# PSUM banks for the last four Q projection pieces of a fused linear-attention and gated-MLP block

## The chip, the cores and the metric

The kernel runs on one core of one Trainium2 chip. The metric is the device time of one execution in microseconds. A core has five instruction streams that run at the same time and meet through semaphores: PE (the matrix engine, with its weight loads listed apart as PEld), DVE (vector), ACT (scalar), POOL, and SP, which here only issues DMAs. Matmuls write into PSUM, which is used as eight banks of 128 partitions x 512 float32; DVE and ACT read the results out of it.

## The reference

`x` is 2048 tokens x 1024 features in bfloat16. The block is a linear attention with 32 heads followed by a gated MLP with 3584 hidden features, each behind a layer norm and each added to the residual:

```
phi(t) = where(t > 0, t + 1, exp(t)) + 1e-6
q, k, v = split(layernorm(x) @ wqkv)            # 32 heads of 32
num = phi(q) @ (phi(k)^T v)     per head
den = phi(q) . sum_s phi(k)     per head, + 1e-6
h   = x + (num / den) @ wo
n   = layernorm(h)
out = h + (relu(n @ W_gate) * (n @ W_up)) @ W_down
```

## The kernel before

**Order of the work.** The program is written as one list of operations per engine (`_Plan`). Every operation names the buffers that it reads and writes, and the planner derives the semaphore waits: a writer waits for all earlier readers and the writer of its buffer, a reader for its writer (lines 50 to 82). Each engine runs its list strictly in the order in which the code adds to it. A PSUM bank is one such buffer (`B_bank[0..7]`), so the first matmul into a bank waits for the engines that last read that bank. All matmuls are recorded at line 453 (`mm`).

**Banks.** `alloc_banks(pool)` (line 330) returns the bank of the given pool that was touched longest ago in program order; it looks at the order in which the program names the banks, not at when they come free. `GB0` is banks 0 to 3, `GB1` banks 4 to 7, `ALL` both.

**Stages.** Tokens are cut into 16 tiles of 128. First come the layer norms, the K projection (two column halves `h`), most of the Q projection, and the attention matrices, up to some 170 us. Tile t's Q piece of half h, `q_piece(t, h, pool)`, is eight matmuls of 128x512 into one bank (`q_mm`, line 629) and an evacuation `phi` in three steps: ACT takes the exponential out of the bank (line 513), DVE clamps it (line 515), and DVE reads the bank again and writes the larger of the two into `pq`, which lies in tile `R_Q` (line 518). The bank is free when the last of these has read it.

**Around the change.** Lines 1046 to 1052 run, in this order on PE: `a4` for token tiles 0 to 3 (two banks each, eight matmuls a bank; the attention output, evacuated by DVE at line 769 with the residual added, then the statistics of the second layer norm, the normalised tile `xn2` in `R_X` and its DMA transpose into `hnT`, line 778), the second half of Q piece (13, 1), and Q pieces (14, 0), (14, 1), (15, 0), (15, 1). Then the MLP begins with round r = 0 (line 1058). `g_unit(r, ft, pair)` (line 782) makes one block of 128 hidden features for 512 tokens: eight matmuls with gate weights into the first bank of its pair, eight with up weights into the second, ACT's relu out of the first (line 801), and DVE's product of both (line 803). The pairs alternate, `pair_of = [(0, 1), (2, 3)]`; the first unit takes banks 0 and 1. Its matmuls read `hnT` of all four tiles of the round, so they also wait for the four DMA transposes of `a4`, and for the first weight blocks. From there on 28 units, two output rounds `d_round` (line 812), and the same for r = 1 to 3 follow; `a4` of the tiles of the next round is put in among the units, on banks 4 to 7.

**Which banks the code gives before the change**, worked through `alloc_banks`: `a4` of tiles 0 to 3 take 5, 4, 3, 2, 0, 6, 7, 5; Q piece (13, 1) holds bank 1; pieces (14, 0), (14, 1), (15, 0), (15, 1) take 4, 3, 2, 0. The later `a4` calls of tiles 4 to 7 take 6, 7, 5, 4, 6, 7, 5, 4.

Of the kernel before, what the change touches and what calls it, by code (L numbers as in the profile page):

```python
# [132 lines left out]
def bass_sequential_preLN__linear_attn_block__glu_gated_reglu__prompt_kernel(  # L133
# [47 lines left out]
    with es:  # L181
# [447 lines left out]
        def q_mm(st, h, pool, b=None, dcs=range(NDC)):  # L629
            if b is None:  # L630
                (b,) = alloc_banks(pool)
            for dc in dcs:
                lhs, bl = (xcT[st][:, dc, :], B_xcT[st][dc // QC]) if st < NC else (xnT[:, st, dc, :], B_xnT[st][dc // HC])
                mm(bank(b), lhs, heads_ji(wq[:, dc, h * NW:(h + 1) * NW]), dc == 0, dc == NDC - 1,
                   [bl, B_wq[h][dc // QC]], B_bank[b], "q_%d_%d" % (st, h))
            return b

        def q_out(st, h, b):
            dst, wb, nm = pq[:, st, h * NW:(h + 1) * NW], [B_pq[st][h]], "q_%d_%d" % (st, h)
            if st < NC:  # L640
                phi_scaled(b, ln1_k[st], dst, wb, nm)
            else:
                phi(b, dst, wb, nm)

        def q_piece(st, h, pool):
            q_out(st, h, q_mm(st, h, pool))
# [218 lines left out]
        GB1 = [4, 5, 6, 7]  # L865
        ALL = GB0 + GB1
# [182 lines left out]
        touch_bank(q13b)  # L1049
        for st in (14, 15):  # L1050
            for h in range(NH):
                q_piece(st, h, ALL)


        BG = [4, 5, 6, 7]
# [78 lines left out]
```

## Time and profile before

| | |
|---|---|
| median of 3 runs | 819.53 us (819.50 to 820.45) |
| the profiled execution, its own time | 820.19 us |
| its span, first to last instruction | 818.4 us |
| granted PE clock | 1.00 |
| PE busy | 811.9 us, 99% of the span, 3960 matmuls |
| DVE busy | 330.5 us, 40% |
| ACT busy | 147.2 us, 18% |
| PE's share of the chain that ended last | 96% |
| DMA queue q1, share of 16 engines' span | 52.4% |

The span is one execution seen by the hardware profiler; what lies around it makes up the rest of that execution's own time. Busy time of PE counts each matmul from its start to its modelled end, and neighbours overlap, so it says that PE is hardly ever without work, not that it works at its peak. An engine's idle time matters only where it lies on the chain of waits that ends last.

### The profile page before, as it was taken

The page shows a single profiled execution, that of the slowest core. Times are in us where ns is not written, and L with a number is a line of the kernel's source. Part 1 is how long each engine was busy: PE and PEld are TensorE (multiplying, and loading weights), DVE is VectorE, ACT ScalarE, POOL GpSimd, SP SyncE. Part 2 cuts the span into 40 slices and gives each one's busy share as a digit, 9 for nine tenths or more (in the row PEclk, how much of TensorE's full clock was granted, in tenths as well). Part 3 has the DMA queues.
Part 4 walks back from the last instruction along what each step waited for, and adds up shares of the span by engine and source line. Part 5 has one row for each costly group of instructions (what it writes and reads, how often), then busy time and mean ns, then how long its engine had stood idle before and what let it go on. Part 6 is the DMA issues. An engine that isn't in the chain of part 4 may idle for free.

```text
span 818.4 us, 9813 instructions
## 1 busy us (share of the span) xinstructions
PE 811.9 (99%) x3960; PEld 369.7 (45%) x3960; DVE 330.5 (40%) x578; ACT 147.2 (18%) x241; POOL 25.5 (3%) x58
## 2 busy tenths in 40 slices
PE   9999999999999999999999999999999999999998
PEld 4444444444444444444444444444444444444444
DVE  7988566675546320155462110554521112211111
ACT  6554323242110110011101100111110001111000
POOL 1221000010000000000000000000000000000000
PEclk9999999999999999999999999999999999999999
DMA  8798000492666546547474655555665553543152
GB/s 238 162 226 211 13 0 1 89 321 55 188 171 168 142 150 197 175 110 229 115 181 142 214 167 171 134 163 141 154 200 166 177 173 107 181 128 103 52 178 79
DMA packets 155357, 122.28 MB, mean 149 GB/s; under 512 B 53936, under 2 KB 150192, under 8 KB 155312
## 3 DMA queue, kind: packets, MB, share of 16 engines
q1 hardware_dynamic: 155168, 121.62, 52.4%
q8 instruction: 31, 0.51, 0.3%
q14 instruction: 14, 0.11, 0.0%
q10 hardware_dynamic: 144, 0.03, 0.0%
HBM read 104.86 MB, written 4.19 MB: 133 GB/s over the span
## 4 chain that ended last, share of the span: by engine, by line
PE 96%; DVE 2%; issue 0%; ACT 0%; DMA 0%; POOL 0%; DVEq 0%; ACTq 0%; POOLq 0%
PE ps L453 96%; DVE st L477 1%; DVE R_Q L769 1%; DVE R_Q L518 0%; DMA R_X<-in_A_x_dram 0%; DVE E2t L515 0%; ACT Et L513 0%; PE ps L588 0%; ACT wo L464 0%; DVE mv L481 0%; DVE pks L837 0%; DVE E2t L566 0%; POOL rstd L490 0%; DVE R_Q L577 0%; DVE ve L487 0%
## 5 line engine op out<-in xcount | busy, mean ns | idle before, releaser
L453 PE MATMUL ps<-R_W,R_N 128*128 128x512 bf16 x1792 | 389.4, 379 | 1.8 <-DVE R_Q L518 1.8
L453 PEld LDWEIGHTS ps<-R_W,R_N 128*128 128x128 bf16 x1792 | 175.3, 98 | 213.5 <-DVE R_Q L518 2.3
L453 PE MATMUL ps<-R_K,R_V 128*128 128x512 bf16 (+1 forms) x924 | 194.1, 373 | 0.0
L803 DVE TENSOR_TENSOR R_V<-R_V,ps 128x512 bf16<-128x512 bf16 x112 | 77.0, 687 | 229.1 <-PE ps L453 229.1
L801 ACT ACTIVATE R_V<-ps 128x512 bf16<-128x512 f32 x112 | 66.9, 597 | 506.6 <-PE ps L453 506.6
L453 PEld LDWEIGHTS ps<-R_K,R_V 128*128 128x128 bf16 x924 | 89.3, 98 | 104.5
L837 DVE TENSOR_TENSOR pks<-ps,R_Q 128x512 bf16<-128x512 f32 (+2 forms) x33 | 20.2, 669 | 176.5 <-PE ps L453 176.5
L453 PE MATMUL ps<-R_K,R_N 128*128 128x512 bf16 x256 | 60.8, 379 | 0.0
L453 PE MATMUL ps<-wo,R_T 128*128 128x512 bf16 x256 | 57.4, 379 | 0.0
L453 PE MATMUL ps<-R_W,R_T 128*128 128x512 bf16 x240 | 56.5, 379 | 0.0
L453 PE MATMUL ps<-R_V,R_T 128*128 128x512 bf16 x224 | 51.0, 379 | 0.0
L513 ACT ACTIVATE Et<-ps 128x512 bf16<-128x512 f32 x58 | 33.9, 594 | 59.2 <-PE ps L453 40.7
L453 PEld LDWEIGHTS ps<-wo,R_T 128*128 128x128 bf16 x256 | 25.0, 98 | 30.2 <-ACT wo L464 0.2
L453 PEld LDWEIGHTS ps<-R_K,R_N 128*128 128x128 bf16 x256 | 24.8, 98 | 30.0 <-issue 0.5
L453 PEld LDWEIGHTS ps<-R_W,R_T 128*128 128x128 bf16 x240 | 23.5, 98 | 28.3
L490 POOL TENSOR_TENSOR rstd<-ve,neghalf 128x1 f32<-128x1 f32 x32 | 18.1, 565 | 562.4 <-DVE ve L487 556.1
L453 PEld LDWEIGHTS ps<-R_V,R_T 128*128 128x128 bf16 x224 | 21.7, 98 | 26.2 <-issue 0.2
L518 DVE SCALAR_TENSOR_TENSOR R_K<-ps,E2t 128x512 bf16<-128x512 f32 x30 | 20.8, 692 | 14.5 <-PE ps L453 13.8
L769 DVE TENSOR_TENSOR R_Q<-ps,x 128x512 bf16<-128x512 f32 x28 | 19.3, 690 | 16.0 <-PE ps L453 16.0
L515 DVE TENSOR_SCALAR E2t<-Et 128x512 bf16<-128x512 bf16 x58 | 16.9, 291 | 14.7 <-ACT Et L513 14.3
L477 DVE BATCH_NORM_STATS2 st<-R_Q 128x6 f32<-128x512 bf16 x32 | 22.2, 694 | 1.1
L622 DVE TENSOR_TENSOR pks<-pks,R_K 128x512 f32<-128x512 f32 x30 | 20.6, 687 | 0.5
(63 smaller groups left out, 233.5 us busy)
## 6 DMA issues: line engine op xcount, KB each, us to landing
R_N<-in_B_W_gate_dram SPq DMA_DIRECT2D x28, 1024.0 KB, 5.4
R_N<-in_B_W_up_dram SPq DMA_DIRECT2D x28, 1024.0 KB, 7.5
R_K<-in_B_W_down_dram SPq DMA_DIRECT2D x56, 512.0 KB, 3.8
R_X<-in_A_x_dram SPq DMA_DIRECT2D x16, 256.0 KB, 3.0
out_dram<-pks SPq DMA_DIRECT2D x31, 128.0 KB, 3.8
x<-in_A_x_dram SPq DMA_DIRECT2D x14, 256.0 KB, 2.8
R_V<-in_A_wqkv_dram SPq DMA_DIRECT2D x8, 256.0 KB, 6.0
R_V<-in_A_wqkv_dram SPq DMA_DIRECT2D x2, 1024.0 KB, 5.9
```

The costliest lines, as they stand in the source:

```text
L453: lambda e: e.matmul(out_ap, lhsT, rhs, start=start, stop=stop, skip_group_check=skip),
L477: PL.add("dve", lambda e: e.bn_stats(out=st6[:, k, c * 6:(c + 1) * 6], in_=src[:, c * BCH:(c + 1) * BCH]), reads=[chunk_bufs[c]], writes=[ ...
L490: PL.add("pool", lambda e: e.tensor_tensor(out=rstd[:, k, :], in0=ve[:, k, :], in1=neghalf[:], op=ALU.pow), reads=[B_ve[k], B_neghalf], wr ...
L513: PL.add("act", lambda e: e.activation(out=Et[:, k, :], in_=src, func=ACTF.Exp), reads=[B_bank[b]], writes=[B_E[k]], name=name + "_exp")
L515: PL.add("dve", lambda e: e.tensor_scalar(out=E2t[:, k, :], in0=Et[:, k, :], scalar1=1.0, scalar2=1e-6, op0=ALU.min, op1=ALU.add), reads=[ ...
L518: PL.add("dve", lambda e: e.scalar_tensor_tensor(out=dst_ap, in0=src, scalar=C1, in1=E2t[:, k, :], op0=ALU.add, op1=ALU.max), reads=[B_ban ...
L622: PL.add("dve", lambda e: e.tensor_tensor(out=pks[:, c], in0=pks[:, c], in1=pk[:, st, :], op=ALU.add), reads=[B_pk[st], B_pks[h]], writes= ...
L769: PL.add("dve", lambda e, b=b, n=n: e.tensor_tensor(out=hsb[:, hs, j, n * NW:(n + 1) * NW], in0=bank(b), in1=x2t[:, n * NW:(n + 1) * NW], ...
L801: PL.add("act", lambda e: e.activation(out=rg[:, k, :], in_=bank(ga, SBW), func=ACTF.Relu), reads=[B_bank[ga]], writes=[B_rg[k]], name="rg ...
L803: PL.add("dve", lambda e: e.tensor_tensor(out=hhT[:, ft, :], in0=rg[:, k, :], in1=bank(gb, SBW), op=ALU.mult), reads=[B_rg[k], B_bank[gb]] ...
L837: PL.add("dve", lambda e: e.tensor_tensor(out=outst[:, k, c0:c1], in0=bank(b, c1 - c0), in1=hsb[:, hs, j, dh * NW + c0:dh * NW + c1], op=A ...
```

## The change

The pool of the last four Q pieces becomes banks 4 to 7 in place of all eight:

```diff
@@ -1049,7 +1049,7 @@
         touch_bank(q13b)
         for st in (14, 15):
             for h in range(NH):
-                q_piece(st, h, ALL)
+                q_piece(st, h, GB1)
```

By `alloc_banks` the pieces (14, 0), (14, 1), (15, 0), (15, 1) now take banks 4, 6, 7, 5 in place of 4, 3, 2, 0, and the `a4` calls of tiles 4 to 7 inside round 0 take 4, 6, 7, 5, 4, 6, 7, 5 in place of 6, 7, 5, 4, 6, 7, 5, 4. No later allocation differs. No instruction is added or removed on any engine, and none changes its place in its engine's order; only bank addresses and semaphore waits differ. On PE two waits move: the first matmul of unit 0 of round 0 keeps its waits for the four transposes and the gate weights, but has none left for ACT and DVE; the first matmul of the same unit's up half, which waited for its weights alone, now waits for ACT and DVE too.

## The prediction

> **What bounds the kernel now.** I read the page's first two parts, then the chain of waits, then PE's waits over time, then the timeline around the one place that these name. The page first:
>
> ```profile
> span 818.4 us, 9813 instructions
> ...
> PE 811.9 (99%) x3960; PEld 369.7 (45%) x3960; DVE 330.5 (40%) x578; ACT 147.2 (18%) x241; POOL 25.5 (3%) x58
> ...
> PE 96%; DVE 2%; issue 0%; ACT 0%; DMA 0%; POOL 0%; DVEq 0%; ACTq 0%; POOLq 0%
> ```
>
> PE is the bound: 96% of the chain that ended last is matmuls. A change of bank can only shorten the run where PE stands still, so the question is where that is. The list of who waited for whom, on PE from 100 us to the end, has one entry:
>
> ```profile
> PE ps L453 <- DVE R_Q L518: 1.8, 1, 1.8
> ```
>
> One stop, 1.8 us, for DVE's last step of `phi`. The chain in order of time puts it:
>
> ```profile
> 190.78 0.31 DVE E2t L515
> 191.11 0.70 DVE R_Q L518
> 191.88 0.60 ACT Et L513
> 192.50 0.30 DVE E2t L515
> 192.83 0.70 DVE R_Q L518
> 193.58 621.41 PE ps L453 x2900
> 815.07 0.44 DVE pks L837
> ```
>
> Up to 193.58 the chain runs through the evacuation of the last Q pieces; from there 621.41 us of matmuls follow without a break, then the last store. So whatever brings the matmul at 193.58 forward brings the end forward by as much. The timeline of PE and its neighbours there:
>
> ```profile
> 187.29 1.23 SPq L778 DMA_TRANSPOSE R_W<-R_X  x1
> ...
> 191.88 0.60 ACT L513 ACTIVATE Et<-ps 128x512 bf16<-128x512 f32 x1 [1.13 <-DVE R_Q L518]
> 192.50 0.29 DVE L515 TENSOR_SCALAR E2t<-Et 128x512 bf16<-128x512 bf16 x1 [0.70 <-ACT Et L513]
> 192.83 0.69 DVE L518 SCALAR_TENSOR_TENSOR R_Q<-ps,E2t 128x512 bf16<-128x512 f32 x1
> 193.58 2.49 PEld L453 LDWEIGHTS ps<-R_W,R_N 128*128 128x128 bf16 x13 [2.28 <-DVE R_Q L518]
> 193.58 2.76 PE L453 MATMUL ps<-R_W,R_N 128*128 128x512 bf16 x12 [1.79 <-DVE R_Q L518]
> ```
>
> The matmul at 193.58 (`R_W` is `hnT`, `R_N` the weight ring) is unit 0 of round 0. It wants bank 0, which piece (15, 1) has just filled; PE must wait for that piece's exponential (191.88 to 192.48), clamp and last read (to 193.52).
>
> **What the change removes.** Piece (15, 1) goes to bank 5, so bank 0's last reader is `a4` of tile 2, first half, the fifth of the eight adds at line 769; in the DVE timeline it starts at 179.52 and takes 0.69 us, over by 180.21. Bank 1, for the up half, is read last by `phi` of piece (13, 1), the first of the five after the norm: 187.50 plus 0.69 is 188.19. Both are done before PE wants them, and the wait of 1.79 us has no bank left to stand on. The exponential, clamp and read still take place, beside the first matmuls of unit 0.
>
> What PE gets is more than the 1.79 us, since that counts from the modelled end of the last Q matmul, and neighbours normally overlap. Pitch: the timeline merges the first 100 matmuls of the MLP to 21.76 us; less one matmul's 0.379, over 99 intervals, 0.216 us. The last Q matmul ends at 193.58 - 1.79 = 191.79 and began at 191.41. With nothing to wait for the next begins at 191.41 + 0.216 = 191.63. Gain: 193.58 - 191.63 = 1.95 us.
>
> **What stands behind the wait.** Unit 0 also reads `hnT` of four tiles and the first weights. The latest transpose is issued at 187.29 (above); the DMA view of 187 to 188.5 us has its landing:
>
> ```profile
> R_W<-R_X SPq DMA_TRANSPOSE x1, 3.6
> ```
>
> 187.29 + 3.6 is 190.9. PE's weight loads run one matmul ahead of their matmuls, so the wait is met at about 191.63 - 0.22 = 191.41: 0.5 us to spare. The same view of the three transposes before gives 4.8 for the first and 3.0 for the third. I take 3.6, the row of this very transfer; bounds are 3.0 (nothing changes) and 4.8, landing at 192.1, which costs 0.7 us. The gate and up weights were issued between 160.18 and 167.4, and the longest median landing of such a block around there is 10.1 us; they are in.
>
> **What it adds.** Four pieces in banks 4, 6, 7, 5 must find these free. Their last readers are the adds of `a4`, tiles 0 (second half), 2 (second half), 3 and 3, which by the DVE timeline end at 175.1, 181.5, 183.4 and 184.8. The pieces start, eight pitches (1.73 us) apart and ending with the one whose last matmul began at 191.41, at 184.72, 186.45, 188.17 and 189.90. Spare: 9.6, 4.9, 4.8 and 5.1 us; cost nothing. If that cover were gone, each late us would stop PE for one.
>
> Next in line: ACT's relu of unit 0 becomes ready 1.95 earlier than 195.57, at 193.62, when the last exponential is over (192.48). DVE's product, at 197.41 before, becomes ready at 195.46, after the last `phi` (193.52). Both gaps could even go: banks 0 and 1 are wanted again only two units on, at 191.63 + 32 x 0.216 = 198.5. Behind SP's last transpose there is no issue before 206.00, which waits for DVE work on unit 2's heels, and weight loads wait for PE to leave a ring slot; so everything after 193.58 moves with PE as one body, and no DMA has to be faster against PE than now. The `a4` calls of tiles 4 to 7 come 14 to 17 units of 3.45 us later; whichever of banks 4 to 7 they take has been free since 193.5. Cost nothing.
>
> Reuse of four banks instead of eight has a row: the first stage rotates its K and Q pieces over banks 4 to 7 with the same evacuations, and in the table by stages, 20 to 60 us, PE is busy 40.00 of 40.00 us at clock 1.00. I take zero for the narrower pool. The Trainium skill speaks against it: "TensorE: Matmul & The Clock Gate", section "A second HAM failure mode: psum-queue depth-cycling", reports a kernel that cycled through PSUM banks, idled in small pieces between groups of matmuls and so had its clock fall back to half again and again. One window of the length that the page gives (some 3.4 us, section "What's actually happening") at half the clock would cost an estimated 1.7 us and leave a gain of 0.25, near 819.3; no run here shows such a fall, and the stage just named contradicts it.
>
> **Sum.** 1.95 gained, 0 given back. The profiled execution would go from 820.19 (span 818.4 and 1.8 around it) to 818.24. That execution lay 0.66 over the median; from 819.53 the same step gives 817.58, so 817.6. About 0.2% (1.64 us) can be told from no change in this kernel; 1.95 is 0.24%, a little over.
>
> **The rivals.**
> *The transpose takes the place of the bank* (chance 0.11). For it: only 0.5 us to spare, and one of four landings took 4.8. Against it: that one was issued while four 512 KB weight loads were under way, and the last is not. At 4.8 the gain is 1.95 - 0.7 = 1.25: 818.3, within 0.2%.
> *The change does not do what it says* (0.04): PE's wait on DVE is a count, and if unit 0 still had to see a late one, say for the up half in bank 1, a part of the stop would come back. Bank 1 is free at 188.19 and wanted at 191.63 + 8 x 0.216 = 193.36, so this needs an error of 5 us in my reading of the order. Then nothing is gained: 819.5.
> *Slower: the pieces wait for their banks* (0.03). Place: the first matmul of (15, 0) in bank 7, which waits for the add of tile 3. Before, bank 2 had been free since 178.3. Price: one us for each us that this add ends after 188.17, less the 1.95 gained; it decides from 190.1 on, 6.7 us later than in this profile. DVE would have to lose that between 173 and 184, where the chain shows it working back to back. A loss of 9 us there gives about 821.8.
>
> **How the numbers follow.** Full gain 0.82, at 817.6; its own range is 817.0 to 818.6, since three runs spread from -0.03 to +0.92 about their median. The transpose's bound of 818.3 and part of its spread carry the range to 819.1; below, there is nothing but noise, some 0.7 us, to 816.9. Left out are mainly the last two rivals and the upper part of the spread. Faster by over 0.2% means under 817.89. The full gain passes that by only 0.3 us, so of its 0.82 I put 0.70 there and 0.12 within; with the transpose and the idle change, of which noise throws 0.01 over the line, within is 0.26 and slower 0.04.
>
> **What would show it.** In the profile after: no entry left on PE for line 518 after 100 us; the first matmul on `R_W`, `R_N` at about 191.6; PE's unbroken run starting before it; the last exponential and `phi` still at 191.9 and 192.8, now under matmuls; a span of about 816.5. An entry on PE for the DMA of `R_W` at 191.6 to 192.1 speaks for the first rival; a PE stop before 191.4 for the third. The prediction is wrong if PE's stop shrinks by clearly less than 1.95, or if it does shrink and a new one opens later in the run.

## The result, and the profile after

Over 13 runs each, the changed kernel takes 817.82 us in the median (817.57 to 818.42) and the kernel before 819.74 us (819.31 to 820.45): 1.92 us less, a ratio of 0.9978 with a 95% interval of 0.9969 to 0.9986. The profiled execution took 817.66 us.

The page of the changed kernel, its span, busy times, the chain by engine, and the group of the MLP's gate and up matmuls (instructions, busy us and mean ns, then idle time before them):

```profile
span 815.9 us, 9813 instructions
...
PE 811.3 (99%) x3960; PEld 369.2 (45%) x3960; DVE 330.0 (40%) x578; ACT 147.0 (18%) x241; POOL 25.7 (3%) x58
...
PE 99%; DMA 0%; DVE 0%; issue 0%; DVEq 0%
...
L453 PE MATMUL ps<-R_W,R_N 128*128 128x512 bf16 x1792 | 389.4, 379 | 0.0
```

The instructions are those of before, and so is the busy time of this group. What differs is its last figure, 0.0 where 1.8 us of idle time for line 518 stood, and PE's share of the chain, 99% instead of 96%: the stretch of DVE and ACT work from 170.6 to 193.6 us has left it.

The chain of waits in order of time (start, us, what), its end:

```profile
6.37 0.63 PE ps L588 x8
7.00 805.60 PE ps L453 x3926
812.60 0.04 DVEq L112
812.63 0.04 issue
812.68 0.46 DVE pks L837
```

One piece of 805.60 us stands where there were two with the evacuations between them. After unit 0 nothing differs: before, 621.41 us passed from its first matmul to the end of PE's work; now it is 7.00 + 805.60 - 191.20 = 621.40 us.

The timeline at the joint, weight loads, matmuls and evacuations:

```profile
190.98 5.49 PEld L453 LDWEIGHTS ps<-R_W,R_N 128*128 128x128 bf16 x26
191.20 5.56 PE L453 MATMUL ps<-R_W,R_N 128*128 128x512 bf16 x25
191.45 0.60 ACT L513 ACTIVATE Et<-ps 128x512 bf16<-128x512 f32 x1 [1.13 <-DVE R_Q L518]
192.08 0.29 DVE L515 TENSOR_SCALAR E2t<-Et 128x512 bf16<-128x512 bf16 x1 [0.71 <-ACT Et L513]
192.41 0.69 DVE L518 SCALAR_TENSOR_TENSOR R_Q<-ps,E2t 128x512 bf16<-128x512 f32 x1
193.17 0.60 ACT L801 ACTIVATE R_V<-ps 128x512 bf16<-128x512 f32 x1 [1.13 <-PE ps L453]
195.02 0.69 DVE L803 TENSOR_TENSOR R_V<-R_V,ps 128x512 bf16<-128x512 bf16 x1 [1.92 <-PE ps L453]
```

The last Q piece is still evacuated, from 191.45 to 193.10, but unit 0 runs meanwhile: its first matmul starts at 191.20, without an idle figure behind it. Its relu and product find ACT and DVE free, as both wait for PE.

This profile's span is 2.5 us shorter, not 1.95. Of the rest, 0.43 us arises before the MLP, and some 0.2 us behind the last matmul: from its start to the end of the span 3.21 us pass before and 3.05 after. The matmuls of the very first K pieces, from 4.5 to 7.2 us, before and then after:

```profile
L453 PE MATMUL ps<-R_W,R_Q 128*128 128x512 bf16 x2 | 0.9, 546 | 0.0
```

```profile
L453 PE MATMUL ps<-R_W,R_Q 128*128 128x512 bf16 x4 | 1.2, 378 | 0.0
```

In the profiled execution before, these matmuls began while PE still ran slowly (546 ns in the mean against 378), and the last 36 Q matmuls begin 0.43 us later (183.86 against 183.43). Up to there both programs are the same, so this belongs to the execution, not to the change (last section).

### The profile page after: what moved, and what is told of

Read it like the earlier page. It is cut to its first block, busy times and chain, and to the rows that moved or that the text cites. A ratio compares the mean times of both kernels' runs of the same rounds, so it can differ in the third digit from the quotient of the medians.

```text
span 815.9 us, 9813 instructions
## 1 busy us (share of the span) xinstructions
PE 811.3 (99%) x3960; PEld 369.2 (45%) x3960; DVE 330.0 (40%) x578; ACT 147.0 (18%) x241; POOL 25.7 (3%) x58
## 4 chain that ended last, share of the span: by engine, by line
PE 99%; DMA 0%; DVE 0%; issue 0%; DVEq 0%
PE ps L453 99%; DMA R_X<-in_A_x_dram 0%; PE ps L588 0%; DVE pks L837 0%; DVE E2t L566 0%; DVE R_Q L577 0%; DVEq L112 0%
```

## The experiments

All six use the changed kernel's text with the lines shown replaced. The pitch is the time from the start of one matmul to the start of the next, 0.216 us (0.2158 to one more digit), and "stop" is the time PE stands still beyond it. In the traces of these six kernels about one matmul record in 50 is missing (74 of 3960), the first of unit 0 among them. In e2, e5 and e6, where the stop is just there, the idle figure in brackets therefore holds one pitch too much, and the stop is worked out from the start of the last 36 Q matmuls: 36 x 0.2158 = 7.77 us later unit 0 is due.

**Only the last piece moves.**

```diff
-        for st in (14, 15):
-            for h in range(NH):
-                q_piece(st, h, GB1)
+        for (st, h), b in zip([(14, 0), (14, 1), (15, 0), (15, 1)], [4, 3, 2, 5]):
+            q_piece(st, h, [b])
```

> Only the last piece, (15, 1), leaves bank 0 and goes to bank 5; the three others keep the banks of before (4, 3, 2). Theory, one bank: unit 0 waits for bank 0 alone, and banks 2 and 3 are wanted only at unit 1, at about 194.7, when the last read of (15, 0) is over at 191.4. So PE has no stop after 100 us and the whole 1.95 us is gained: about 817.8. Rival, the narrow pool as such: pieces (14, 1) and (15, 0) in banks 3 and 2 hold unit 1 up, PE keeps a stop of 0.5 us or more there, and less than 1.5 us is gained.

Measured: 817.78 us against 819.81 before, ratio 0.9976 (0.9966 to 0.9986). The list of who waited for whom has no entry on PE for DVE, ACT or a DMA after 100 us, only three short gaps (0.5 us together, the longest 0.2) that every one of the six traces with missing records shows:

```profile
PE ps L453 <- issue: 0.5, 3, 0.2
```

Unit 0's first record is at 191.39, one pitch after the 191.17 at which it was due, as its first matmul is the missing one: no stop. The other three pieces, back in banks 4, 3 and 2, cost nothing: within the interval the whole gain is one piece in one bank, and the narrow pool as such does nothing that can be told.

**The last piece back in bank 0**, the others as changed. The edit is that of e1 with

```diff
+        for (st, h), b in zip([(14, 0), (14, 1), (15, 0), (15, 1)], [4, 6, 7, 0]):
```

> The first three pieces as in the changed kernel (4, 6, 7), the last one back in bank 0. Theory, one bank: the stop of 1.8 us for the last read of phi at unit 0 is back in full, time within 0.1% of before, about 819.7. Rival, the gain came from the other three pieces or from an earlier start of the run (0.43 of the 2.5 us by which the two spans differ lie before the MLP): the stop is smaller than 1 us and at least 0.5 us of gain stays.

Measured: 819.76 us against 819.81, ratio 0.9999 (0.9990 to 1.0008). The timeline of PE:

```profile
183.32 7.93 PE L453 MATMUL ps<-R_V,R_T 128*128 128x512 bf16 x36
193.27 4.05 PE L453 MATMUL ps<-R_W,R_N 128*128 128x512 bf16 x18 [2.02 <-DVE R_Q L518]
```

Unit 0 was due at 183.32 + 7.77 = 191.09 and began one pitch before the record at 193.27, at 193.05: a stop of 1.96 us, the one of before (1.95). The profiled execution of e2 also began early (its Q matmuls start 0.54 us sooner than in the profile before), and it took 819.58 us, no less than the fastest of the 30 runs of before (819.54). So an early start of this size doesn't give the gain.

**The last piece in bank 1**, which unit 0 wants eight matmuls later:

```diff
+        for (st, h), b in zip([(14, 0), (14, 1), (15, 0), (15, 1)], [4, 6, 7, 1]):
```

> As the changed kernel, but the last piece in bank 1, which unit 0 wants eight matmuls later, for its up half. Theory, one bank and its time: wanted at 191.20 + 1.73 = 192.93, last read over at 193.10, so PE stops 0.2 us (a pitch of about 0.45 us in place of 0.216, shown as some 0.1 us idle) and 1.7 us is gained: about 818.0. Rival, any bank of unit 0 costs the whole wait: the stop is 1.5 us or more and nothing is gained.

Measured: 818.50 us against 819.81, ratio 0.9983 (0.9974 to 0.9992). PE's timeline:

```profile
191.56 5.80 PE L453 MATMUL ps<-R_W,R_N 128*128 128x512 bf16 x25
```

25 matmuls at the pitch take 24 x 0.2158 + 0.379 = 5.56 us; here they take 5.80, so there is a stop of about 0.23 us inside, too short to be listed as a wait of PE. The weight loads show where it lies and for what:

```profile
193.29 0.76 PEld L453 LDWEIGHTS ps<-R_W,R_N 128*128 128x128 bf16 x5 [0.56 <-DVE R_Q L518]
```

It lies at the first matmul of the up half, right behind the end of the last read at 193.24. That is the stop the theory gave, and the rival's 1.5 us is not there. The time is 0.5 us above the figure expected, which the interval (817.7 to 819.2) allows; what else may lie in it isn't settled.

**The last but one piece in bank 0:**

```diff
+        for (st, h), b in zip([(14, 0), (14, 1), (15, 0), (15, 1)], [4, 6, 0, 5]):
```

> The last but one piece, (15, 0), takes bank 0 and the last one bank 5 (banks 4, 6, 0, 5). Theory, one bank and its time: bank 0 is read to 191.37 and wanted at 191.20, so PE stops 0.2 us at unit 0 (a pitch of some 0.44 us) and 1.7 us is gained: about 818.1. Rival, any of the four pieces in bank 0 holds the MLP up until the whole evacuation is over: the stop is 1.8 us as before, 819.8.

Measured: 818.12 us against 819.90, ratio 0.9979 (0.9970 to 0.9989).

```profile
183.50 7.93 PE L453 MATMUL ps<-R_V,R_T 128*128 128x512 bf16 x36
191.72 5.56 PE L453 MATMUL ps<-R_W,R_N 128*128 128x512 bf16 x25 [0.29 <-DVE R_Q L518]
```

Due at 191.27, begun at 191.72 - 0.22 = 191.50: a stop of 0.23 us, as expected (the last read ended at 191.44, 0.17 us after unit 0 was due). It isn't bank 0 that costs 1.95 us, but how late its last reader is when PE comes to it.

**Two banks for four pieces**, which makes the third wait for the first:

```diff
+        for (st, h), b in zip([(14, 0), (14, 1), (15, 0), (15, 1)], [4, 6, 4, 6]):
```

> The four pieces take banks 4, 6, 4, 6: the pool is narrowed once more, so that (15, 0) must wait for the last read of (14, 0). Theory: that read ends at 188.68 and the piece wants its bank at 187.74, so PE stops 1.0 us before the MLP (some 0.8 us idle for line 518), the later reads are in time, and half the gain is left: about 818.8, still with no stop at unit 0. Rival, the pieces have enough time in any two banks: no stop, 817.8. Rival, a late piece starts a chain in which each of the following waits again: two stops or more, over 819.7.

Measured: 818.96 us against 819.81, ratio 0.9989 (0.9980 to 0.9998).

```profile
183.50 4.48 PE L453 MATMUL ps<-R_V,R_T 128*128 128x512 bf16 x20
188.81 3.63 PE L453 MATMUL ps<-R_V,R_T 128*128 128x512 bf16 x16 [0.83 <-DVE R_Q L518]
192.49 4.70 PE L453 MATMUL ps<-R_W,R_N 128*128 128x512 bf16 x21
```

One stop, at (15, 0): due at 183.50 + 20 x 0.2158 = 187.82, begun at 188.81, 0.99 us. The fourth piece and unit 0 follow without another. The read that it waited for, of piece (14, 0), ended at 188.75, 0.93 us after PE was due. This is the slower rival's mechanism, with another late reader, on the chip and nearly at its stated price, one for one; two banks are too few, four are enough (three were not run).

**The transpose made late**: one 512 KB load put on the DMA queue ahead of it.

```diff
             if 4 <= st + 2 < NST:
                 load_x2(st + 2)
+            if st == STB - 1:
+                load_wd_next()
...
-        for _ in range(NWS):
+        for _ in range(NWS - 1):
             load_wd_next()
```

> The changed kernel with one of the four first down-weight loads (512 KB) taken from ahead of the a4 calls and put on the DMA queue just before the last transpose of hnT, which unit 0 needs. Theory: with the bank wait gone the transpose is next in line, and it has about 0.5 us to spare (landing near 190.3 here, its first reader's weight load at 190.98). 512 KB at the 360 GB/s that the queue reached earlier are 1.4 us, and its issue takes some 0.5 us more, so the transpose lands at about 191.6 to 192.2, PE stops 0.6 to 1.2 us for a DMA into R_W, and the time is 818.4 to 819.0. Rival, more room than that or transfers that do not queue behind each other: no stop on PE, 817.8.

Measured: 818.66 us against 819.90, ratio 0.9983 (0.9974 to 0.9993). PE's timeline, and the landing of the last transpose (issued at 187.82):

```profile
184.18 7.93 PE L453 MATMUL ps<-R_V,R_T 128*128 128x512 bf16 x36
192.68 4.70 PE L453 MATMUL ps<-R_W,R_N 128*128 128x512 bf16 x21 [0.56 <-DMA R_W<-R_X]
```

```profile
R_W<-R_X SPq DMA_TRANSPOSE x1, 4.6
```

It lands at 187.82 + 4.6 = 192.4. Unit 0 was due at 191.95 and began at 192.46: a stop of 0.51 us, and the one wait listed for PE after 100 us, besides the three short gaps, is now for this DMA. So the transpose is next in line behind the bank. Counted from the first of the 36 Q matmuls it lands at 8.23 us here and at 6.82 in the changed kernel (190.25 - 183.43): the load ahead puts it off by 1.4 us, more than its room. That the stop is not larger has a reason in the rows: after a stop the first matmul starts with its weight load, not a pitch behind it (before: both at 193.58), so the room for the matmul in the changed kernel is 191.20 - 190.25 = 0.95 us, of which the weight load's lead of 0.22 us is a part. The stop is a little under the 0.6 to 1.2 us expected; the time is inside what was.

Put together, stop and gain add up to 1.5 to 2.0 us throughout, which is the same within the intervals (some 0.8 us to either side of each gain), as it must be if the stop is all there is:

| kernel | stop on PE, us | gain over before, us | sum |
|---|---|---|---|
| before | 1.95 | 0 | 1.95 |
| e2, last piece in bank 0 | 1.96 | 0.05 | 2.01 |
| e4, two banks | 0.99 | 0.85 | 1.84 |
| e5, transpose late | 0.51 | 1.24 | 1.75 |
| e6, last but one in bank 0 | 0.23 | 1.78 | 2.01 |
| e3, last piece in bank 1 | 0.23 | 1.31 | 1.54 |
| e1, only the last piece moved | 0 | 2.03 | 2.03 |
| the change | 0 | 1.92 | 1.92 |

## Why the prediction was right

The time forecast, 817.6 us, started from a median of three runs, 819.53; over 13 runs the median of before is 819.74, and the changed kernel's 817.82 lies 1.92 us below that. That the gain is over 0.2% isn't settled, as the interval of the ratio, 0.9969 to 0.9986, has 0.9980 inside.

*PE stands still once, for bank 0.* Right: e2 puts the stop back with that one bank, and e1 takes it away with that one piece. Of the four pieces named in the change three need not have moved.

*The gain is the idle figure plus the overlap.* Predicted 1.95 us; the start of unit 0 against the last 36 Q matmuls moved forward by 1.95 us, from 193.58 - 183.86 = 9.72 to 191.20 - 183.43 = 7.77, and the medians by 1.92. The 1.79 us shown as idle alone would have been short by the overlap of two neighbours.

*The transpose has 0.5 us to spare.* Right in order and nearly in size. In the profile after it was issued at 186.85 and took

```profile
R_W<-R_X SPq DMA_TRANSPOSE x1, 3.4
```

so it landed near 190.25, some 0.7 us ahead of the weight load at 190.98. The rival built on the 4.8 us landing didn't come about in that profile, but e5 shows that a late landing stops PE: there it took 4.6 us, from an issue 0.2 us later against the Q matmuls. The spare time was counted to the weight load, though, and e5 shows that the matmul can start together with it; an estimate from that is 0.2 us more room, and a price of about 0.5 us in place of 0.7 for a landing of 4.8.

*Pieces in banks 4, 6, 7, 5 find them free.* Right: no stop before unit 0. The price given for the case that they don't, one for one, is nearly what e4 measured, 0.99 us of stop for a read 0.93 us late.

*Nothing later gives the gain back.* Right: 621.40 us after unit 0's first matmul, against 621.41. The chain after is PE alone from 7.00 to 812.60 us, so no DMA there came to hold it; that they moved with PE because they wait for it was read from the program, not tested.

*The clock does not fall for the narrow pool.* The clock record of the profile after is one stretch of 812.37 us at full clock, and the 805.60 us on the chain have no gap. What the Trainium skill's page "TensorE: Matmul & The Clock Gate", section "A second HAM failure mode: psum-queue depth-cycling", reports of a kernel that cycled through PSUM banks did not come about here: in that kernel PE idled briefly between groups of matmuls again and again, and here it does not.

*The span.* Predicted 816.5, profiled 815.9. The step that was missing is mainly the start of the run: the prediction took it to be the same in both profiles, and it was 0.43 us slower before than after. That the profiled execution before was slow, 0.66 us over its median, was taken as noise; the lengths of its first matmuls would have shown a slow start, though not how much of the 0.66 us it makes up.

## What to carry to other kernels

A rotation that picks the bank touched longest ago in program order looks back only; it doesn't see which bank the next stage wants first. Look at where a stage begins with fixed banks, and keep the last piece before it out of the first of those. What such a stop costs is the lateness of the last reader when the next matmul is due, not the whole evacuation; here it was paid in full, as PE bounds the kernel. Before counting a removed wait as gain, find what the same instruction waits for next and by how much; here it was a DMA transpose that landed 0.95 us before its matmul was due.

## What the runs showed of the hardware

The start of the run moves later work by more than expected. PE's clock is granted in full at some point in the first microseconds: by the clock record of the traces at 6.67 us in the profile before, 5.00 after, 4.03 in e1, 4.52 in e2, 6.01 in e3, 4.00 in e4, 7.38 in e5 and 4.95 in e6. The record has no entry ahead of that, and the tables by stages print 1.00 there all the same; the length of the matmuls (546 against 378 ns above) shows the slower clock. Where the grant came at 5.00 us or sooner, the last 36 Q matmuls begin between 183.32 (e2) and 183.50, in no order; where it came later they begin later, at 183.57 in e3, 183.86 before and 184.18 in e5. Between the ends lie 0.86 us. The 13 runs of the changed kernel spread by 0.85 us. That the start accounts for this spread is an inference, since only the profiled executions show their clock.

The full clock lasted 812.37 us in seven of the eight traces and 808.96 in e5, 3.41 us less. The Trainium skill's page "TensorE: Matmul & The Clock Gate", section "What's actually happening", says that the gate works in windows of some 3.4 us that run freely and do not begin with the kernel; the step of 3.41 us and the scattered grant agree with that, and no run here tests it further.

From the end of DVE's last read to PE's first matmul behind it passed 0.06 us (before: 193.52 to 193.58), and from the landing of the transpose in e5 about as much (192.41 to 192.46, the start worked out as above).
